# A fused attention and feed-forward kernel whose instructions are placed by a planner at build time, with a first batch in two query halves

## The chip, the cores and the metric

The kernel runs on one core of one Trainium2 chip. The metric is the device time in microseconds (us). The profile shows one execution; its span is about 1.8 us shorter than the time of the same run. Engines are written as in the profile: PE is TensorE, PEld its weight loads, DVE is VectorE, ACT is ScalarE, POOL is GpSimd, SP is SyncE. A tile is a named buffer; a bank is a piece of the memory that matmuls write to. The profile also records the clock that the array is granted, here full or half. "L84" is line 84 of the kernel that was profiled, so the numbers differ from one kernel to the next.

## The reference

Eight batches of squared-relu attention (12 heads, 448 tokens, head size 64), then an RMS norm and a gated feed-forward layer over 3584 tokens:

```python
scores = scale * np.matmul(q, k.transpose(0, 1, 3, 2))
attn = np.maximum(scores, 0.0) ** 2 / S
x = np.matmul(attn, v)                       # then heads side by side: 3584 x 768
xn = x / np.sqrt(np.mean(x * x, -1, keepdims=True) + 1e-06) * rms_g
g = xn @ w_gate                              # 768 -> 1536
out = (g * sigmoid(g) * (xn @ w_val)) @ w_out    # 1536 -> 768
```

## The kernel before

While the feed-forward layer of batch b runs on the PE, the attention of batch b+1 is put between its matmuls at fixed shares of the work. Nearly all matmuls use 64 of the 128 rows, so that two run side by side, one on each row half. Batch 0 has nothing to hide behind, so its whole attention and norm come first. Matmuls on zeros ("fillers", `psB`) keep the array busy there. All fillers of one call write one tile:

```python
def keep_busy(n):
    ps = ps_m.tile([P, S], FP32, name="psB", tag="mm")
    for _ in range(n):
        nc.tensor.matmul(out=ps[:], lhsT=ones_bf[:], rhs=busy_bf[:], start=True, stop=True)
...
keep_busy(16)
for _, fn in attention(0) + [(1.1, lambda: norm(0))]:
    fn()
keep_busy(24)
for nm in ("q", "k", "v"):
    load(nm, 1)
load_wo(0, 2)
load_wo(1, 2)
for b in range(B):
    ...                                # feed-forward of b, attention of b + 1 between
```

The norm of a batch is a square root on ACT, a reciprocal on DVE and six scalings on DVE:

```python
nc.scalar.activation(out=rstd[:], in_=psSS[:, :S], func=ACT.Sqrt, scale=1.0 / float(DM), bias=eps_col[:])
act_table(ACT.Silu)
nc.vector.reciprocal(out=rstd[:], in_=rstd[:])
```

Of the kernel before, what the change touches and what calls it, by code (L numbers as in the profile page):

```python
# [9 lines left out]
I32 = mybir.dt.int32  # L10
# [4 lines left out]
NCH = 4  # L15
U = 7
UH = 4


@with_exitstack  # L20
def kernel(
# [19 lines left out]
    assert HP == KT and (2 * S) % P == 0  # L41
    eps = 1e-6
    inv_attn = 1.0 / (float(D) * float(S))
    NT = 2 * S // P

# [6 lines left out]
    apool = ctx.enter_context(tc.tile_pool(name="attn", bufs=12))  # L52
    xpool = ctx.enter_context(tc.tile_pool(name="xT", bufs=1))
    npool = ctx.enter_context(tc.tile_pool(name="norm", bufs=2))
    hpool = ctx.enter_context(tc.tile_pool(name="hT", bufs=2))
    spool = ctx.enter_context(tc.tile_pool(name="sig", bufs=3))
    opool = ctx.enter_context(tc.tile_pool(name="ostage", bufs=3))
    ps_s = ctx.enter_context(tc.tile_pool(name="ps_s", bufs=2, space=bass.MemoryType.PSUM))
    ps_m = ctx.enter_context(tc.tile_pool(name="ps_m", bufs=4, space=bass.MemoryType.PSUM))
# [3 lines left out]
    ld = {}  # L63
    qkT = {}
    src_of = {"q": q, "k": k, "v": v}
    PE_T = 2

    def load(nm, b, h0=0, h1=H):
        runs = nm == "v" or b < PE_T
        n, w = (PC, NCH) if nm == "q" else (P, UH)  # L70
        if (nm, b) not in ld:
            shape = [n, H, w * D] if runs else [n, w, H * D]
            ld[nm, b] = ldpool.tile(shape, BF16, name=nm + "b", tag=nm + "b")
            if nm == "k" and runs:
                nc.vector.memset(ld[nm, b][D:, :, (UH - 1) * D :], 0.0)
        t = ld[nm, b]
        src = src_of[nm][b, h0:h1]
        if nm == "q":
            parts = [(slice(0, PC), PC, 0, NCH)]
        else:  # L80
            parts = [(slice(0, D), D, 0, UH), (slice(D, P), D, UH if nm == "k" else UH - 1, U)]
        for prt, n, u0, u1 in parts:
            if runs:
                nc.gpsimd.dma_start(  # L84
                    out=t[prt, h0:h1, : (u1 - u0) * D],
                    in_=src.rearrange("h (p u) d -> p h (u d)", p=n)[:, :, u0 * D : u1 * D],
                )
            else:
                to = t[prt].rearrange("p u (h d) -> p u h d", d=D)
                rows = src.rearrange("h (p u) d -> p u h d", p=n)  # L90
                step = u1 - u0 if nm == "q" else 1
                for u in range(u0, u1, step):
                    nc.gpsimd.dma_start(  # L93
                        out=to[:, u - u0 : u - u0 + step, h0:h1, :], in_=rows[:, u : u + step]
                    )

    def new_qkT(b):
        qkT[b] = qtpool.tile([P, HP, 2, S], BF16, name="qkT", tag="qkT")

    def transpose_dma(b):  # L100
        new_qkT(b)
        for c in range(UH):
            n = P if c < UH - 1 else D
            nc.sync.dma_start_transpose(
                out=qkT[b][:, :, 0, c * P : c * P + n], in_=ld["k", b][:n, c, :]
            )
        for c in range(NCH):
            nc.sync.dma_start_transpose(
                out=qkT[b][:, :, 1, c * PC : (c + 1) * PC], in_=ld["q", b][:, c, :]
            )  # L110

    wg_sb = wpool.tile([P, KT, F], BF16, name="wg_sb", tag="wg")
    wv_sb = wpool.tile([P, KT, F], BF16, name="wv_sb", tag="wv")
    wo_sb = wpool.tile([P, FT, DM], BF16, name="wo_sb", tag="wo")
    NSL = 4
    FS = F // NSL

    def load_w(which, s):
        dst, src = {"g": (wg_sb, moe_w_gate), "v": (wv_sb, moe_w_val)}[which]
        nc.gpsimd.dma_start(  # L120
            out=dst[:, :, s * FS : (s + 1) * FS],
            in_=src.rearrange("(kt p) f -> p kt f", p=P)[:, :, s * FS : (s + 1) * FS],
        )

    def load_wo(s, n):
        w = FT // n
        nc.gpsimd.dma_start(
            out=wo_sb[:, s * w : (s + 1) * w, :],
            in_=moe_w_out.rearrange("(fk p) m -> p fk m", p=P)[:, s * w : (s + 1) * w, :],
        )  # L130

    ones_bf = const.tile([P, P], BF16, name="ones_bf", tag="ones_bf")
    nc.vector.memset(ones_bf[:], 1.0)
    busy_bf = const.tile([P, S], BF16, name="busy_bf", tag="busy_bf")
    nc.vector.memset(busy_bf[:], 0.0)  # L135

    def keep_busy(n):
        ps = ps_m.tile([P, S], FP32, name="psB", tag="mm")
        for _ in range(n):
            nc.tensor.matmul(out=ps[:], lhsT=ones_bf[:], rhs=busy_bf[:], start=True, stop=True)  # L140

    load("q", 0, 0, 2)
    load("k", 0, 0, 2)
    ident = const.tile([P, P], BF16, name="ident", tag="ident")
    masks.make_identity(nc, ident[:])
    eps_col = const.tile([P, 1], FP32, name="eps_col", tag="eps_col")
    nc.vector.memset(eps_col[:], eps)
    scrap = const.tile([P, 1], FP32, name="scrap", tag="scrap")

    def act_table(func):  # L150
        nc.scalar.activation(out=scrap[:], in_=eps_col[:], func=func)

    act_table(ACT.Sqrt)
    g_sb = wpool.tile([P, KT], FP32, name="g_sb", tag="rmsg")
    nc.sync.dma_start(out=g_sb[:], in_=moe_rms_g.rearrange("(kt p) -> p kt", p=P))
    load("q", 0, 2, 6)
    load("k", 0, 2, 6)
    load("v", 0, 0, 6)
    load("q", 0, 6, 12)
    load("k", 0, 6, 12)  # L160
    load("v", 0, 6, 12)
    for s in range(NSL):
        load_w("g", s)
        load_w("v", s)

    behind = mybir.DependencyInfo(mybir.DependencyClass.Sync, mybir.DependencyReason.DATA)
    xTs = {}

    def transposes(b, j):
        if j == 0:  # L170
            new_qkT(b)
        psT = ps_m.tile([P, 2, S], BF16, name="psT", tag="mm")
        flat = psT[:].rearrange("p t s -> p (t s)")
        for nm, n, w, at in (("k", P, UH, 0), ("q", PC, NCH, S)):
            for c in range(w):
                for hh in range(2):
                    nc.tensor.transpose(  # L177
                        out=flat[hh * D : (hh + 1) * D, at + c * n : at + (c + 1) * n],
                        in_=ld[nm, b][:, 2 * j + hh, c * D : (c + 1) * D],
                        identity=ident[:n, :n],  # L180
                    )
        nc.vector.tensor_copy(out=qkT[b][:, j, :, :], in_=psT[:])

    rsq = {}
    pending = []

    def relu_on(b, j, c):
        return "dve" if c == UH - 1 or (b and j % 2 and c == 2) else "act"

    def square_on(b, j, c):  # L190
        return "pool" if b == 0 and j >= 3 and c == 1 else "dve"

    def flush():
        while pending:
            pending.pop(0)()

    def rectify(b, j, c, psS):
        r = apool.tile([P, 2, S], BF16, name="r", tag="r")
        if relu_on(b, j, c) == "dve":
            nc.vector.tensor_relu(out=r[:], in_=psS[:, :, :S])  # L200
        else:
            nc.scalar.activation(out=r[:], in_=psS[:, :, :S], func=ACT.Relu)  # L202
        eng = nc.gpsimd if square_on(b, j, c) == "pool" else nc.vector
        flush()
        pending.append(lambda: eng.tensor_tensor(out=r[:], in0=r[:], in1=r[:], op=ALU.mult))  # L205
        rsq[b, j, c] = r

    def scores(b, j, c):
        psS = ps_s.tile([P, 2, 512], FP32, name="psS", tag="psS")
        for hh in range(2):  # L210
            prt = slice(hh * D, (hh + 1) * D)
            nc.tensor.matmul(  # L212
                out=psS[:, hh, :S],
                lhsT=qkT[b][prt, j, 0, c * P : (c + 1) * P],
                rhs=qkT[b][prt, j, 1, :],
                start=True,
                stop=True,
            )
        rectify(b, j, c, psS)

    def rest_scores(b, j):

        psS = ps_s.tile([P, 2, 512], FP32, name="psS", tag="psS")
        for hh in range(2):
            prt = slice(hh * D, (hh + 1) * D)
            for jj in range(2):
                nc.tensor.matmul(  # L227
                    out=psS[jj * D : (jj + 1) * D, hh, :S],
                    lhsT=qkT[b][prt, j + jj, 0, (UH - 1) * P : (UH - 1) * P + D],
                    rhs=qkT[b][prt, j + jj, 1, :],  # L230
                    start=True,
                    stop=True,
                )
        return psS

    x2s = {}

    def attend(b, j, then=None):
# [35 lines left out]
        if then:  # L274
            rectify(*then, UH - 1, psR)
# [27 lines left out]

    xns, hTs = {}, {}

    class Stream:



# [270 lines left out]
```

## Time and profile before

| | before |
|---|---|
| time, median of 3 runs | 468.07 us (467.43 to 469.23) |
| span of the profiled run | 466.5 us |
| first projection matmul starts | 45.4 us |
| last matmul ends | 461.5 us |
| PE, DVE, ACT busy | 97%, 59%, 50% |

The page of the kernel before: the busy line, the chain that ended last, and two groups (busy us and mean ns of one after the bar, then the idle time before them):

```profile
PE 453.6 (97%) x5722; PEld 292.8 (63%) x5722; DVE 274.0 (59%) x403; ACT 234.9 (50%) x360; POOL 80.6 (17%) x97
...
PE 91%; DVE 3%; ACT 2%; DMA 1%; POOL 1%; issue 1%; POOLq 0%
...
L424 DVE RECIPROCAL rstd<-rstd 128x448 f32<-128x448 f32 x8 | 23.6, 2953 | 26.0 <-ACT rstd L420 26.0
...
L140 PE MATMUL psB<-busy_bf,ones_bf 128*128 128x448 bf16 x58 | 17.6, 418 | 1.3 <-DVE busy_bf L135 1.3
```

The timeline of the same run on PE (start us, length us, engine, line, what, count, and in brackets the idle time before it):

```profile
1.30 5.36 PE L140 MATMUL psB<-busy_bf,ones_bf 128*128 128x448 bf16 x16 [1.30 <-DVE busy_bf L135]
6.59 0.41 PE L177 MATMUL psT<-ident,kb 128*64 128x128 bf16 x8
...
9.59 0.64 PE L177 MATMUL psT<-ident,kb 128*64 128x128 bf16 x8 [2.39 <-DMA kb<-in_k_dram]
...
45.38 0.38 PE L441 MATMUL psP<-xn,wg_sb 128*64 128x448 bf16 x2
```

The same eight transposes take 0.41 us at 6.59 us, when the array's clock is full, and 0.64 us at 9.59 us, when the trace has it at half (from 9.1 to 19.4 us). PE is the chain, and it is busy 97% of the span. But that busy time contains 17.6 us on zeros, and the first useful projection starts only at 45.38 us.

Busy time does not tell how full the array is, because matmuls overlap. So I use one more measure, worked out from the start of every matmul in the trace. A matmul of N columns takes a slot, 189 ns for 448 columns, 109 ns for 256 and 96 ns for 224 (these are the spacings of adjacent starts). A matmul on half or a quarter of the array counts for half or a quarter of a slot. "Lost" is the length of a stretch less the slots of the useful matmuls that start in it. Fillers are not useful. The last matmul is counted to the end of its slot, 461.3 us before. Before, the useful slots sum to 405.6 us, and 33.8 us are lost before the first projection. A steady batch later loses only 2.4 to 2.9 us.

### The profile page before, as it was taken

What the parts mean: (1) busy time and instruction counts of PE and PEld (TensorE: products, weight loads), DVE (VectorE), ACT (ScalarE), POOL (GpSimd) and SP (SyncE); (2) the same over time, 40 slices, a digit from 0 to 9 for tenths busy, and PEclk for the clock granted to TensorE, in tenths of its full rate; (3) what the DMA queues carried; (4) which work ended last, traced back from release to release, by engine and by line L of the source; (5) the groups of instructions that cost most, each with busy time, mean ns of one, the idle gap of its engine ahead of it and who ended that gap; (6) DMA issues with size and microseconds to landing.
All of it is one profiled execution on the core that took longest, in us unless ns stands there. A gap on an engine that the chain in (4) does not pass through costs nothing.

```text
span 466.5 us, 12798 instructions
## 1 busy us (share of the span) xinstructions
PE 453.6 (97%) x5722; PEld 292.8 (63%) x5722; DVE 274.0 (59%) x403; ACT 234.9 (50%) x360; POOL 80.6 (17%) x97
## 2 busy tenths in 40 slices
PE   6989999999999999999999999999999999999995
PEld 3434655676666766676666766676667766676674
DVE  1676378866663867576566657576656677332200
ACT  1682246665645655375445755465535764532221
POOL 8438211571007000340007000100000000000000
PEclk8698999999999999999999999999999999999998
DMA  9999999799907970299209960438002200020013
GB/s 106 194 204 199 206 173 162 80 204 165 127 3 107 214 124 2 23 200 146 44 1 124 211 109 1 58 82 135 20 1 54 85 2 1 2 84 20 1 42 95
DMA packets 130758, 44.47 MB, mean 95 GB/s; under 512 B 102928, under 2 KB 127120, under 8 KB 130704
## 3 DMA queue, kind: packets, MB, share of 16 engines
q0 software_dynamic: 91648, 24.39, 54.1%
q1 hardware_dynamic: 39056, 19.28, 20.5%
q8 instruction: 44, 0.72, 0.6%
q14 instruction: 10, 0.08, 0.0%
HBM read 48.76 MB, written 11.01 MB: 128 GB/s over the span
## 4 chain that ended last, share of the span: by engine, by line
PE 91%; DVE 3%; ACT 2%; DMA 1%; POOL 1%; issue 1%; POOLq 0%
PE psP L380 47%; PE psO L380 23%; PE psAV L258 8%; PE psS L212 6%; PE psSS L380 2%; ACT r L202 2%; PE psB L140 1%; PE psT L177 1%; PE psS L227 1%; DMA kb<-in_k_dram 1%; DVE xn L427 1%; PE psP L441 1%; DVE r L200 1%; DVE r L205 1%; DVE rstd L424 1%
## 5 line engine op out<-in xcount | busy, mean ns | idle before, releaser
L380 PE MATMUL psP<-xn,wv_sb 64*128 64x448 bf16 x1140 | 229.0, 349 | 0.0
L380 PE MATMUL psP<-xn,wg_sb 64*128 64x448 bf16 x1128 | 227.8, 349 | 0.1
L380 PE MATMUL psO<-wo_sb,hT 64*128 64x256 bf16 x2016 | 139.6, 271 | 0.0
L202 ACT ACTIVATE r<-psS 128x896 bf16<-128x896 f32 x123 | 111.1, 918 | 47.5 <-PE psS L212 46.8
L380 PEld LDWEIGHTS <-wv_sb 64*128 64x128 bf16 x1140 | 96.1, 94 | 41.5 <-issue 4.3
L380 PEld LDWEIGHTS <-hT 64*128 64x128 bf16 x2016 | 101.1, 94 | 33.0 <-issue 2.9
L380 PEld LDWEIGHTS <-wg_sb 64*128 64x128 bf16 x1128 | 94.3, 94 | 35.6 <-issue 1.3
L205 DVE TENSOR_TENSOR r<-r 128x896 bf16<-128x896 bf16 x165 | 100.9, 628 | 16.3 <-ACT r L202 15.6
L456 DVE TENSOR_TENSOR hT<-sil,psP 128x448 bf16<-128x448 bf16 x96 | 59.5, 620 | 79.7 <-PE psP L380 52.4
L451 ACT ACTIVATE sil<-psP 128x448 bf16<-128x448 f32 x96 | 51.9, 542 | 74.7 <-PE psP L380 68.8
L200 DVE TENSOR_SCALAR r<-psS 128x896 bf16<-128x896 f32 x45 | 49.1, 1090 | 31.7 <-PE psS L227 24.2
L212 PE MATMUL psS<-qkT 64*128 64x448 bf16 x288 | 59.3, 358 | 1.9 <-DVE r L200 1.2
L490 ACT COPY ost<-psO 128x256 f32<-128x256 f32 x84 | 30.5, 372 | 43.5 <-PE psO L380 39.6
L276 ACT ACTIVATE xT<-psAV 128x896 bf16<-128x896 f32 x24 | 22.0, 917 | 54.4 <-PE psAV L258 50.1
L258 PE MATMUL psAV<-r,vb 64*64 64x448 bf16 x672 | 43.9, 361 | 1.8 <-POOL r L205 1.2
L84 POOL DMA_DIRECT2D vb<-in_v_dram x18 | 13.2, 750 | 167.7 <-PE psO L380 122.3
L424 DVE RECIPROCAL rstd<-rstd 128x448 f32<-128x448 f32 x8 | 23.6, 2953 | 26.0 <-ACT rstd L420 26.0
L93 POOL DMA_DIRECT2D kb<-in_k_dram x42 | 33.0, 1008 | 18.7 <-DMA wo_sb<-in_moe_w_out_dram 9.6
L258 PEld LDWEIGHTS <-vb 64*64 64x64 bf16 x672 | 17.3, 106 | 22.3 <-issue 10.3
L427 DVE SCALAR_TENSOR_TENSOR xn<-xT,g_sb,rstd 128x448 bf16<-128x448 bf16 x48 | 29.3, 680 | 0.3
L212 PEld LDWEIGHTS <-qkT 64*128 64x128 bf16 x288 | 19.8, 94 | 11.4 <-issue 6.2
L140 PE MATMUL psB<-busy_bf,ones_bf 128*128 128x448 bf16 x58 | 17.6, 418 | 1.3 <-DVE busy_bf L135 1.3
(38 smaller groups left out, 161.7 us busy)
## 6 DMA issues: line engine op xcount, KB each, us to landing
vb<-in_v_dram POOLq DMA_DIRECT2D x14, 384.0 KB, 7.2
qb<-in_q_dram POOLq DMA_DIRECT2D x7, 672.0 KB, 12.9
kb<-in_k_dram POOLq DMA_DIRECT2D x43, 96.0 KB, 12.7
out_dram<-ost SPq DMA_DIRECT2D x8, 336.0 KB, 4.1
wg_sb<-in_moe_w_gate_dram POOLq DMA_DIRECT2D x4, 576.0 KB, 16.5
wv_sb<-in_moe_w_val_dram POOLq DMA_DIRECT2D x4, 576.0 KB, 18.1
wo_sb<-in_moe_w_out_dram POOLq DMA_DIRECT2D x2, 1152.0 KB, 21.4
out_dram<-ost SPq DMA_DIRECT2D x8, 288.0 KB, 4.4
```

What stands on the lines that cost most here:

```text
L93: nc.gpsimd.dma_start(out=to[:, u - u0 : u - u0 + step, h0:h1, :], in_=rows[:, u : u + step])
L200: nc.vector.tensor_relu(out=r[:], in_=psS[:, :, :S])
L202: nc.scalar.activation(out=r[:], in_=psS[:, :, :S], func=ACT.Relu)
L205: pending.append(lambda: eng.tensor_tensor(out=r[:], in0=r[:], in1=r[:], op=ALU.mult))
L212: nc.tensor.matmul(out=psS[:, hh, :S], lhsT=qkT[b][prt, j, 0, c * P : (c + 1) * P], rhs=qkT[b][prt, j, 1, :], start=True, stop=True,)
L258: mm = nc.tensor.matmul(out=psAV[hh * D : (hh + 1) * D, jj, :S], lhsT=v[prt, 2 * (j + jj) + hh, u * D : (u + 1) * D], rhs=r[prt, hh, :], s ...
L380: mm = nc.tensor.matmul(out=self.ps[:, : self.w], lhsT=self.lhsT(i)[prt], rhs=self.rhs(i)[prt], start=(half == 0 and i == 0), stop=(half = ...
L424: nc.vector.reciprocal(out=rstd[:], in_=rstd[:])
L427: nc.vector.scalar_tensor_tensor(out=xn[:, kt, :], in0=xTs[b][:, kt, :], scalar=g_sb[:, kt : kt + 1], in1=rstd[:], op0=ALU.mult, op1=ALU.mult,
L451: nc.scalar.activation(out=s[:], in_=psG[:], func=ACT.Silu)
L456: nc.vector.tensor_tensor(out=hTs[b // 2][:, fb, o : o + S], in0=sil[b, fb][:], in1=psV[:], op=ALU.mult)
L490: nc.scalar.copy(out=ost[:, o : o + w], in_=ps[:, :w])
```

## The change

The intent is twofold. A planner with a model of every engine's times decides, while the kernel is built, in what order each engine gets its instructions and which engine takes a movable one. And batch 0 attends in two halves of 224 queries each: the first half is normed and goes through eight of the twelve pairs of projections before the second half is through. The diff has 1693 lines and rewrites the body of the kernel; this is its core, cut:

```diff
+class Bank:
+    def take(self, name, dtype=FP32, shape=None):
+        self.free = None
+        return self.pool.tile(shape or self.shape, dtype, name=name, tag=self.tag)
+class Planner:
+    SEM, PSUM, HAND, SW = 50.0, 210.0, 200.0, 95.0
...
+    def filler(self):
+        self.row()
+        s = max(self.t)
+        self.fill()
+        self.t = [s + 96.0, s + 96.0]
...
+    subs = [Sub(0, 0, HALF, 0.0), Sub(0, HALF, HALF, 0.0)]
+    subs += [Sub(b, 0, S, 0.0 if b < 2 else PACE) for b in range(1, B)]
...
+        cost = {"dve": dve_cost(2 * w, 0.52)}
+        if sub.b < 2:
+            cost["pool"] = 156.0 + 1.75 * 2 * w        # squares of batches 0 and 1
+        pl.task(PRIO_R, cost, square, [a], tok)
...
-        nc.vector.reciprocal(out=rstd[:], in_=rstd[:])
+                out=rstd[:, q0 : q0 + n], in_=rstd[:, q0 : q0 + n], func=ACT.Exp, scale=-0.5
...
+    def fill():
+        free = [x for x in wide + banks if x.free is not None and x.free <= max(pl.t)]
+        if not free:
+            return False
+        ps = free[0].take("psB")
+        o = ps[:, 0, :HALF] if free[0] in wide else ps[:, :HALF]
+        nc.tensor.matmul(out=o, lhsT=ones_bf[low, :], rhs=busy_bf[low, :], start=True, stop=True)
+        free[0].free = max(pl.t) + 96.0
+        return True
```

A filler is now 224 columns on the lower 64 rows, and every one takes a new tile of the first free bank. `Planner` assumes 96 ns for each.

## The prediction

> **What bounds it now.** A head, then a TensorE that hardly stops. In the timeline the first projection starts at 45.4 us, after the whole first batch: transposes from 6.6 us, scores, relu, squares, output, then a norm of sqrt, reciprocal (2.95 us on VectorE) and six scalings of 0.68 us. From 45.4 to 461.5 us TensorE is never named idle; copy and DMA end the span at 466.5 us. The chain of waits is 91% TensorE. I count each matmul as one row-tile slot: 189 ns (448 columns) or 109 ns (256), the spacing of adjacent starts in the timeline. The matmuls then fill 95% of each later period between first projections of consecutive batches (48.5 of 51.1 us), and 90% of 45 to 100 us. So the steady part can give about 2.5 us per batch; the head far more.
>
> **What changes.** The built order shows the same useful matmul work: 405.6 us of slots before, 406.0 after, without fillers. Batch 0 attends in two query halves; the first half's norm and first eight projection pairs come before the second half is through. Only 9.4 us of slots precede the first projection. The reciprocal becomes Ln and Exp: 0.6 us of Exp and a table load instead of 2.95 us. The Trainium skill (ScalarE: Activation LUTs, "What ACT_TABLE_LOAD costs") gives about 1283 ns per load; the trace shows 1283. Loads rise from 16 to 27. Each output-projection group hands over between row halves once, not twice; a handover costs two slots 11 ns each, so 84 fewer save about 2 us.
>
> **Head.** 57 fillers of 224 columns run first. The skill (TensorE: Matmul & The Clock Gate, Part 1) says the array starts at half clock, needing a busy window of about 3.4 us; the trace grants full clock at 5.7 us. At 187 ns cold and 96 ns warm they end near 9 us, 2 us later than the transposes start now. Half 1 then needs, by the order and the trace's durations (relu 0.92 or 1.09, square 0.62, copies 0.5 to 0.7, half widths 0.4 to 0.6), some 16 us on each of ScalarE and VectorE, plus about 3 us of waits: first projection at about 28.5 us (26 to 32) instead of 45.4.
>
> **After it.** 390.8 us of slots remain; at 95.5% 409 us. About 1.5 us more because 224-wide matmuls leave less time to load weights, and about 2 us because half 2's scaling (10 to 12 us of VectorE work) outlasts half 1's projections (about 10 us). Tail 5 us. Span 28.5 + 409 + 3.5 + 5 = 446; with the offset from span to time, 1.6 us, about 447; fewer handovers may take 1 to 2 us off: **446 us, range 440 to 454**. Chances: faster by over 2% 0.92, within 2% 0.06, slower 0.02.
>
> **What would show it.** Timeline: first gate projection at 26 to 32 us. Windows: slots fill 95 to 97% of the steady periods. Groups: no reciprocal; 27 table loads. Waits: TensorE waits about 2 us for scaling between 35 and 45 us. Last matmul to end of span still 5 us.
>
> **What would make it wrong.** A static order built on a model of time: if real fillers, DMAs or clock lag it, in-order engines stand; half-array fillers might not release the clock, moving the first projection past 32 us; half 2 could starve TensorE for 5 us or more; if the steady part lost more to placement than to switching and weight loads, the result is below 440.

## More of the kernel before

The squares of the scores go to POOL for three tiles of batch 0 only. POOL also issues all loads:

```python
def square_on(b, j, c):
    return "pool" if b == 0 and j >= 3 and c == 1 else "dve"
```

## The result, and the profile after

| | before | changed |
|---|---|---|
| time, median | 467.75 us (4 runs) | 492.61 us (4 runs, 492.58 to 495.26) |
| ratio, 95% interval | | 1.0549 (1.0495 to 1.0604) |
| span of the profiled run | 466.5 us | 490.8 us |
| first transpose on PE | 6.6 us | 23.7 us |
| first projection | 45.4 us | 59.9 us |

The change is 5% slower, where 5% faster was predicted.

The page of the changed kernel, the lines that answer to those of before. The last row is from its second part, PE clock in tenths by slices of 12.3 us:

```profile
PE 471.3 (96%) x6110; PEld 314.9 (64%) x6110; DVE 252.7 (51%) x413; ACT 260.7 (53%) x388; POOL 85.3 (17%) x100
...
PE 88%; DMA 4%; ACT 2%; issue 1%; DVE 1%; SPq 1%; POOL 1%; ACTq 0%
...
L1214 PE MATMUL psB<-busy_bf,ones_bf 64*128 64x224 bf16 x122 | 38.6, 322 | 6.9 <-DVE eps_col L390 1.2
...
PEclk9999989999899999999999999999999999999998
```

Its timeline in the head, PE lines, with two of the weight loads between the fillers:

```profile
1.18 22.56 PE L1214 MATMUL psB<-busy_bf,ones_bf 64*128 64x224 bf16 x57 [1.18 <-DVE eps_col L390]
...
1.58 0.10 PEld L1214 LDWEIGHTS <-ones_bf 64*128 64x128 bf16 x1 [0.30 <-issue]
1.98 0.10 PEld L1214 LDWEIGHTS <-ones_bf 64*128 64x128 bf16 x1 [0.29 <-issue]
...
23.67 0.64 PE L580 MATMUL psT<-ident,kb 128*64 128x128 bf16 x8
...
59.88 0.45 PE L138 MATMUL psg<-xn,wg_sb 64*128 64x224 bf16 x3
```

The 57 fillers last from 1.18 to 23.7 us: 396 ns each, not 96. The page calls PE busy in that time, and the list of waits names none, because the wait lies between two instructions of PE itself. The sign of it is the weight load that sits idle 0.30 us for "issue" before every filler. The built program says why: 112 of the 122 fillers wait on PE's own semaphore for the matmul just before. Two tiles of one bank follow each other, so the second must wait until the first is written and released.

The clock row is misleading here. The trace holds its first clock entry at 46.8 us, and the page shows full clock for the time before it. Yet eight transposes at 23.67 us take 0.64 us, as in the half-clock stretch of the kernel before (at 9.59 us), not 0.41 us. And the fillers themselves stand 396 ns apart there, but 308 ns at the end of the head, once the trace has full clock. I take it that the array ran at half clock until the first entry.

The waits of PE in the changed kernel (us in total, times, longest), and the chain behind the first of them (start us, us, what):

```profile
PE psR L735 <- DMA qkT<-qb: 4.8, 1, 4.8
PE psB L1214 <- DVE eps_col L390: 1.2, 1, 1.2
PE psS L714 <- DVE r L657: 1.0, 1, 1.0
```

```profile
98.43 1.78 POOL r L665
100.21 0.62 POOL kb L477
100.95 0.74 POOL kb L477
101.68 11.72 DMA qb<-in_q_dram
113.42 1.27 SPq L615
114.73 2.21 SPq L615
116.98 2.72 SPq L615
119.75 9.27 DMA qkT<-qb
129.05 0.59 PE psR L735 x4
```

Batch 2's q was loaded too late: its issue stands on POOL behind a square (`r L665`) of batch 1. A half-clock window begins as the stall ends, at 128.7 us.

Where the time went, in lost us by stretch (useful slots: 405.6 before, 406.0 in the others). Two repaired kernels of the experiments are shown with them:

| lost us | before | changed | E3 | E5 |
|---|---|---|---|---|
| until the first projection | 33.8 | 50.8 | 22.4 | 21.6 |
| to the first projection of batch 1 | 5.4 | 8.9 | 7.3 | 6.5 |
| to that of batch 2 | 2.9 | 9.0 | 9.5 | 2.7 |
| from there to the last matmul | 13.7 | 11.1 | 11.1 | 11.0 |
| after the last matmul | 5.2 | 5.1 | 5.2 | 5.2 |
| span | 466.5 | 490.8 | 461.4 | 453.1 |

The steady part did gain: the stretch from batch 2's first projection on loses 2.6 us less. The loss lies in the head (17.0 us), in the stretch after it (3.5) and in the one that holds the stall before batch 2's attention (6.1).

### The profile page after: what moved, and what is told of

Read it like the earlier page. It is cut to its first block, busy times and chain, and to the rows that moved or that the text cites. A ratio compares the mean times of both kernels' runs of the same rounds, so it can differ in the third digit from the quotient of the medians.

```text
span 490.8 us, 13609 instructions
## 1 busy us (share of the span) xinstructions
PE 471.3 (96%) x6110; PEld 314.9 (64%) x6110; DVE 252.7 (51%) x413; ACT 260.7 (53%) x388; POOL 85.3 (17%) x100
## 4 chain that ended last, share of the span: by engine, by line
PE 88%; DMA 4%; ACT 2%; issue 1%; DVE 1%; SPq 1%; POOL 1%; ACTq 0%
PE psv L138 22%; PE psg L138 21%; PE psO L138 20%; PE psB L1214 8%; PE psAV L821 8%; PE psS L714 6%; DMA qb<-in_q_dram 2%; DMA qkT<-qb 2%; PE psT L580 2%; PE psSS L138 2%; SPq L615 1%; PE psR L735 1%; DVE xn L920 1%; ACT r L659 1%; POOL r L665 0%
## 5 line engine op out<-in xcount | busy, mean ns | idle before, releaser
L138 PE MATMUL psg<-xn,wg_sb 64*128 64x448 bf16 (+1 forms) x1248 | 235.8, 338 | 0.5 <-DVE xn L920 0.5
L138 PE MATMUL psv<-xn,wv_sb 64*128 64x448 bf16 (+1 forms) x1248 | 235.2, 337 | 0.0
L665 DVE TENSOR_TENSOR r<-r 128x896 bf16<-128x896 bf16 (+1 forms) x166 | 101.5, 627 | 28.7 <-ACT r L659 28.1
L995 DVE TENSOR_TENSOR hT<-sil,psv 128x448 bf16<-128x448 bf16 x96 | 59.4, 619 | 56.1 <-PE psv L138 56.0
L982 ACT ACTIVATE sil<-psg 128x448 bf16<-128x448 f32 x96 | 52.0, 542 | 43.4 <-PE psg L138 43.2
L714 PE MATMUL psS<-qkT 64*128 64x448 bf16 (+1 forms) x324 | 62.6, 346 | 1.5 <-DVE r L657 1.0
L1214 PE MATMUL psB<-busy_bf,ones_bf 64*128 64x224 bf16 x122 | 38.6, 322 | 6.9 <-DVE eps_col L390 1.2
L821 PE MATMUL psAV<-r,vb 64*64 64x448 bf16 (+1 forms) x756 | 43.8, 340 | 0.3
L657 DVE TENSOR_SCALAR r<-psS 128x896 bf16<-128x896 f32 x22 | 23.9, 1089 | 28.1 <-PE psS L714 27.4
L920 DVE SCALAR_TENSOR_TENSOR xn<-xT,g_sb,rstd 128x448 bf16<-128x448 bf16 (+1 forms) x54 | 30.2, 627 | 5.8 <-ACT rstd L905 5.8
L821 PEld LDWEIGHTS <-vb 64*64 64x64 bf16 x756 | 18.7, 107 | 20.2 <-PE psAV L821 8.4
L1214 PEld LDWEIGHTS <-ones_bf 64*128 64x128 bf16 x122 | 12.4, 103 | 28.0 <-issue 26.2
```

The lines of the kernel that those rows point to most:

```text
L138: mm = self.nc.tensor.matmul(out=seg.bank["tile"][:, off : off + seg.w], lhsT=lhsT[prt], rhs=rhs[prt], start=(seg.first and h == 0 and i = ...
L657: nc.vector.tensor_relu(out=r[:, :, :w], in_=ps[:, :, :w])
L665: eng.tensor_tensor(out=r[:, :, :w], in0=r[:, :, :w], in1=r[:, :, :w], op=ALU.mult)
L714: nc.tensor.matmul(out=ps[:, hh, o : o + n], lhsT=t[prt, j, 0, c * P : (c + 1) * P], rhs=t[prt, j, 1, sub.q0 : sub.q0 + n], start=True, st ...
L821: mm = nc.tensor.matmul(out=ps[hh * D : (hh + 1) * D, jj, :n], lhsT=vt[prt, 2 * (ja + jj) + hh, u * D : (u + 1) * D], rhs=r[prt, hh, o : o ...
L920: nc.vector.scalar_tensor_tensor(out=xn[:, kt, q0 : q0 + n], in0=xTs[b, 0][:, kt, q0 : q0 + n], scalar=g_sb[:, kt : kt + 1], in1=rstd[:, q ...
```

## The experiments

The theories: (A) each filler waits for the one before, and that is the lost head. (B) The rival: fillers on half of the rows do not release the clock. (C) A second rival, the one that the prediction itself named: a static order lags the real machine everywhere, and the fillers are incidental. Later, for the stall: (D) POOL's squares hold up the loads; (E) other transfers at the same time slow them.

### E1 to E4: the wait and the rows, each alone and both; and no fillers

E1 keeps the tile while the bank's last user was a filler. Of 112 waits for PE itself 1 is left, and every other instruction keeps its place:

```diff
-        ps = free[0].take("psB")
+        ps = free[0].held if free[0].name == "psB" else free[0].take("psB")
```

> Same order on every engine as the changed kernel; the 122 half-array fillers keep one PSUM tile while nothing else used the bank, so 1 instead of 112 of them waits for the matmul before it. Theory A (each filler waits for the completion of the one before, 396 ns apart instead of 96 to 187): 57 fillers end at 7 to 12 us instead of 23.7, first gate projection at 29 to 36 us instead of 59.9, time 455 to 470 us (the 5 us wait for batch 2's transposed q may grow). Rival B (the 64-row fillers never release the clock, whatever their spacing): fillers end at 11 to 12 us, transposes still take 0.64 us per eight, clock full only from 35 us or later, time 465 to 475. Rival C (the static order as such lags, fillers incidental): time stays above 485.

E2 leaves the waits and uses all rows; E3 has both edits:

```diff
-        nc.tensor.matmul(out=o, lhsT=ones_bf[low, :], rhs=busy_bf[low, :], ...)
+        nc.tensor.matmul(out=o, lhsT=ones_bf[:], rhs=busy_bf[:], ...)
```

> Same order, fillers use all 128 rows, and each still takes a new tile and so waits for the one before. Theory A: 57 fillers still take 15 to 23 us, first gate projection at 45 to 60 us, time 478 to 493. Rival B (half-array fillers are what kept the clock at half until 46.8 us): clock full before 10 us, transposes 0.41 us per eight, time 470 to 485.

> Both mended: full-array fillers in one tile. Theory A and B together: fillers end at 8 to 12 us, clock full by 8 us and held, first gate projection at 27 to 32 us, time 448 to 462 with the wait for batch 2's transposed q at 5 us or more. If A alone matters, equal to the half-array version within 3 us. Rival C: above 485.

E4 has no fillers:

```diff
     def warm():
...
-        return 0 not in started
+        return False
```

> No fillers at all; the array waits for its data. Theory A: transposes start at 6.5 to 7.5 us; clock at half through most of the head; first gate projection at 30 to 37 us; time 452 to 470. Rival B (the clock matters more than the fillers' own time): time 475 or more, because the whole head runs at half clock. Rival C: above 485.

| | fillers' rows | wait | time us | ratio to before | clock first full at | first transpose | first projection |
|---|---|---|---|---|---|---|---|
| changed | 64 | yes | 492.61 | 1.0549 | 46.8 us | 23.7 | 59.9 |
| E1 | 64 | no | 471.43 | 1.0074 | 15.4 us | 11.9 | 34.4 |
| E2 | 128 | yes | 496.79 | 1.0633 | 48.7 us | 23.9 | 62.2 |
| E3 | 128 | no | 462.82 | 0.9901 | 6.9 us | 9.5 | 31.5 |
| E4 | none | | 463.64 | 0.9900 | 16.4 us | 6.4 | 29.5 |

The heads of E1, E2 and E3, in this order, from their timelines:

```profile
1.18 10.79 PE L1217 MATMUL psB<-busy_bf,ones_bf 64*128 64x224 bf16 x57 [1.18 <-DVE eps_col L393]
11.90 0.64 PE L583 MATMUL psT<-ident,kb 128*64 128x128 bf16 x8
```

```profile
22.78 1.14 PE L1214 MATMUL psB<-busy_bf,ones_bf 128*128 128x224 bf16 x3
23.86 0.64 PE L580 MATMUL psT<-ident,kb 128*64 128x128 bf16 x8
```

```profile
1.18 8.37 PE L1217 MATMUL psB<-busy_bf,ones_bf 128*128 128x224 bf16 x57 [1.18 <-DVE eps_col L393]
9.48 0.41 PE L583 MATMUL psT<-ident,kb 128*64 128x128 bf16 x8
```

A holds. Taking the wait away takes 21.2 us off (492.61 to 471.43), with every instruction in its old place, so C cannot explain the slowdown. The rows alone (E2) gain nothing: with the wait, fillers on all rows do not release the clock either, until 48.7 us. So B fails as the rival cause. It is a second, smaller cause once the wait is gone: E3 beats E1 by 8.6 us, with the clock full at 6.9 us instead of 15.4, and the transposes at 0.41 instead of 0.64 us. E4 says how bad the fillers of the changed kernel are: without any it is 29 us faster than with them. Three expected times were missed by a little: E1 lies 1.4 us above A's range, E3 1 us, and E2 4 us. The stall is still in all four: waits of 4.2 to 7.3 us in their profiles.

### E5 and E6: the late load of batch 2

E5 is E3 with batch 1's squares off POOL:

```diff
-        if sub.b < 2:
+        if sub.b < 1:
             cost["pool"] = 156.0 + 1.75 * 2 * w
```

> Full-array fillers in one tile (462.8 us before this) and, besides, batch 1's squares never on GpSimd, whose queue also issues the loads. Theory D (batch 2's loads stand behind those squares in GpSimd's order, so the transposed q is 5.6 us late and the stall costs a half-clock window): the q load is issued at 52 to 60 us instead of 71.7, no wait of TensorE on it, no clock drop at 99 us; time 453 to 458. Rival E (the transfers of batch 3's loads, running at the same time, make the q load and the transposes slow): q still 2 us or more late, time 459 to 463.

E6 is E3 with batch 3's loads planned 20 us later:

```diff
-            load_later(b + 2, [Tok(max(pl.t))])
+            load_later(b + 2, [Tok(max(pl.t) + (20000.0 if b == 1 else 0.0))])
```

> Full-array fillers in one tile, and batch 3's loads planned 20 us later, squares left on GpSimd. Rival E: q load of batch 2 takes 8 to 10 us instead of 12.6 and its last transpose 4 to 5 us instead of 8.9; wait under 1 us; time 455 to 459. Theory D alone: the load still starts at 71 us, the wait shrinks by 2 us at most; time 460 to 463.

E5: 455.05 us (4 runs, 454.49 to 455.30), ratio 0.9721 (0.9703 to 0.9738), 7.8 us less than E3. POOL in E3 and then in E5, the square and the loads of batch 2:

```profile
68.40 1.78 POOL L668 TENSOR_TENSOR r<-r 128x896 bf16<-128x896 bf16 x1 [5.23 <-ACT r L662]
70.14 1.53 POOL L480 DMA_DIRECT2D kb<-in_k_dram  x2
71.65 2.31 POOL L480 DMA_DIRECT2D qb<-in_q_dram  x1
```

```profile
58.48 0.75 POOL L480 DMA_DIRECT2D kb<-in_k_dram  x1 [4.82 <-DMA wo_sb<-in_moe_w_out_dram]
64.80 2.27 POOL L480 DMA_DIRECT2D qb<-in_q_dram  x1 [5.58 <-PE psAV L824]
```

And the longest wait of PE in E3, then in E5:

```profile
PE psR L738 <- DMA qkT<-qb: 5.4, 1, 5.4
```

```profile
PE psS L717 <- ACT xT L849: 1.4, 1, 1.4
```

The q load is issued 6.85 us sooner (71.65 to 64.80). The wait of 5.4 us is gone, and with it the half-clock window that E3's trace has at 99.0 us. The load itself is no faster: it lands 12.6 us after its issue in E3 (at 84.2 us) and 12.4 us after it in E5 (at 77.2). But the four transposes of q that follow it are faster. Their line in the DMA view of E3 and then of E5 (the last number is the median us from issue to landing):

```profile
qkT<-qb SPq DMA_TRANSPOSE x4, 9.1
```

```profile
qkT<-qb SPq DMA_TRANSPOSE x4, 5.6
```

The last of them lands at 99.55 us in E3 and at 87.27 in E5. Of these 12.3 us, 7.0 come from the earlier load, which is D. The other 5.2 come from faster transposes: in E3 five loads of batch 3 are issued at 75.1 to 79.2 us, just before them, and in E5 these loads come only from 85.4 us on, after the last of the transposes was issued (84.5). That is what E would lead to. As an estimate from these numbers, either part alone would have covered nearly all of the wait of 5.4 us. So E5 shows what the squares on POOL cost in this plan, but not how much of it goes by D and how much by E. The Trainium skill (TensorE: Matmul & The Clock Gate, Part 1, on engine queue depths) gives GpSimd strict FIFO order, per core of that engine; this case agrees: the load stood behind a square that itself waited 5.23 us. E5's load came later than I expected (52 to 60 us), since something else then held it until 64.8.

E6 failed as an experiment. The order of POOL's instructions came out the same as E3's, and the loads of batch 3 still followed directly. At 463.63 us (ratio 0.9913) it is in effect a repeat of E3, with a wait of 7.2 us in its profile. It was meant to part D from E, so that question stays open.

### E7, E10: the first batch whole

E7 is E3 with one sub-batch for batch 0 and one norm; E10 has the squares off POOL too, so it compares with E5.

```diff
-    subs = [Sub(0, 0, HALF, 0.0), Sub(0, HALF, HALF, 0.0)]
+    subs = [Sub(0, 0, S, 0.0)]
...  (loads of q, transposes and the projections' order go with it)
```

> Full-array fillers in one tile and the planner, but the first batch attends whole, with one norm and full-width projections. If the halves are worth what the prediction gave them (first projection about 17 us sooner, some 10 us of it paid back by work that moves behind it): first projection at 40 to 46 us, time 468 to 476. If the planner alone carries the gain: within 3 us of 462.8.

> The first batch whole, with the q load no longer late. If the two halves are worth about what they save in lost time (22.4 + 16.8 us lost up to batch 3 with halves, 27.3 + 10.9 + 1.5 without, both with a wait of 5 us): time 456 to 460, first projection at 39 to 41 us, no wait for the transposed q. If the halves matter more: 461 to 468.

E7: 464.54 us, ratio 0.9931, first projection at 40.2 us. E10: 458.04 us, ratio 0.9788 (0.9763 to 0.9812), first projection at 39.7 us. So the halves bring the first projection 9 us forward (30.8 in E5) but are worth only 3.0 us in the end (458.04 to 455.05), because the second half's attention and more lost time follow it: E5 loses 6.5 us in the next stretch, E10 4.8. My first range for E7 (468 to 476) was too high; the other one, within 3 us of 462.8 if the planner alone carries the gain, held. Most of the gain of the repaired kernels is not that of the halves: E10 is 10.2 us below the 468.26 us of the kernel before in its rounds. That is the rest of the diff, the planned order and the norm without the reciprocal among it; no run separates these.

### E8: the wait put into the kernel before

```diff
         for _ in range(n):
+            if last is not None:      # wait for the completion of the filler before
+                tc.add_manual_dep(nc.tensor.nop().ins, last.name, ...)
-            nc.tensor.matmul(out=ps[:], ...)
+            last = nc.tensor.matmul(out=ps[:], ...).ins
```

> The kernel before, with nothing changed but that each filler of a run of fillers waits for the one before it. Theory A: the first 16 take about 9 us instead of 5.4 (585 ns apart cold), the 24 ahead of the first projection about 8 to 9 us instead of 4.7 if warm and 13 if cold; first projection at 50 to 58 us instead of 45.4; time 473 to 482. If the wait costs nothing by itself: 466 to 470.

E8: 475.47 us, ratio 1.0145 (1.0116 to 1.0174). Its first fillers and transposes, to be compared with 5.36 and 0.41 us before:

```profile
1.29 9.73 PE L144 MATMUL psB<-busy_bf,ones_bf 128*128 128x448 bf16 x16 [1.29 <-DVE busy_bf L135]
10.96 0.64 PE L181 MATMUL psT<-ident,kb 128*64 128x128 bf16 x8
```

The fillers stand 613 ns apart at half clock instead of 373, and 423 ns at full clock instead of 189. The first projection comes at 53.0 us instead of 45.4, and the clock is full only from 21.4 us instead of 5.7. After the head, every stretch loses the same as before, within 0.2 us. So the wait costs this much in a kernel without the planner as well; it shows A independently of everything else in the change. The size is E8's own: here the weight load also stands behind the wait, and in the changed kernel it does not.

### E9, E11, E12: how much the fillers are worth

All three start from E5. E9 puts the fillers back on 64 rows, with the tile kept. E11 plans 150 ns for a filler, which leaves 37 before the first transpose and 79 in all. E12 has none. The edits in this order:

```diff
-        nc.tensor.matmul(out=o, lhsT=ones_bf[:], rhs=busy_bf[:], ...)
+        nc.tensor.matmul(out=o, lhsT=ones_bf[low, :], rhs=busy_bf[low, :], ...)
```

```diff
-        self.t = [s + 96.0, s + 96.0]
+        self.t = [s + 150.0, s + 150.0]
```

```diff
-        return 0 not in started
+        return False
```

> The kernel of 455.05 us (full-array fillers in one tile, batch 1's squares off GpSimd) with its fillers back on 64 rows; the tile is still kept. Theory B' (64 rows release the clock later: 15.4 us against 4.4 to 6.9 us in the profiles so far): clock full at 10 to 20 us, fillers end at 10 to 12 us instead of 8.5, first projection 2 to 4 us later, time 457 to 465. If the rows do not matter and the earlier difference was the phase of the clock's windows: 454 to 457 and clock full by 8 us.

> The kernel of 455.05 us, planned with 150 ns for a filler instead of 96, so 37 instead of 57 fillers come first and 79 instead of 122 in all. If the first fillers still outlast the arrival of data: first transpose at 6.5 to 7.5 us instead of 8.7, time 452.5 to 454.5. If the clock falls to half for it: 455 to 460.

> The kernel of 455.05 us without any filler. Theory: the head is bound by ScalarE and VectorE, so a half clock there costs little: first projection at 29 to 31 us, time 453 to 458. If a half clock matters: 459 or more.

| | time us | ratio to before | first projection | half clock after its first release, in the profile |
|---|---|---|---|---|
| E5 | 455.05 | 0.9721 | 30.8 us | none until the end |
| E9 | 461.01 | 0.9862 | 37.2 us | none, but first full at 22.0 us |
| E11 | 455.74 | 0.9737 | 29.7 us | 29.8 to 36.6 us |
| E12 | 457.01 | 0.9763 | 29.7 us | 24.6 to 34.8 us |

E9 confirms the rows by themselves: 6.0 us, and in both profiles with fillers on 64 rows and no wait the clock was released only after the first run of fillers had ended at 12.0 us (at 15.4 and 22.0 us, against 4.4 to 6.9 us in all seven profiles with fillers on 128 rows and no wait: E3, E5, E6, E7, E10, E11 and E13). E11 came out in its second range: its first projection came 1 us sooner, but the half clock then fell into the projections, and the stretch to batch 1 lost 10.5 us instead of 6.5. E12 shows the same without fillers. Good fillers are worth about 2 us here (457.01 to 455.05, in different rounds), and 0.8 us, within the noise, from E4 to E3; those of the changed kernel cost 29 (463.64 in E4 to 492.61).

### E13, E14: what was left open

E13 is E5 with only the first run of fillers shortened to 37. E14 is the changed kernel with only E5's edit, the squares.

```diff
-        self.t = [s + 96.0, s + 96.0]
+        w = 96.0 if self.real else 150.0      # real: set by the first transpose
+        self.t = [s + w, s + w]
```

> The kernel of 455.05 us, with 37 instead of 57 fillers before the first transpose and the later ones planned at 96 ns as there (65 of them). If the clock fell in the trimmed kernel because the later fillers thinned out (65 to 42): clock held at full from about 6 us, first transpose at 7 us, first projection at 29 to 30 us, time 453 to 454.5. If a shorter first run alone is enough to lose the clock: a half-clock window between 20 and 40 us, time 455 to 458.

> The changed kernel as it stands, fillers untouched, only batch 1's squares taken off GpSimd. Theory D holds without the filler repair too: no wait of TensorE for the transposed q, saving 5 to 9 us: 484 to 488. If the fillers' delay is what makes the loads late here: within 2 us of 492.6.

E13: 453.91 us, ratio 0.9712 (0.9683 to 0.9742), the best of all, but its interval overlaps that of E5. Its profile has the first transpose at 6.4 us, and one half-clock window from 31.8 to 35.2 us. So whether the thinner later fillers or the shorter first run cost E11 the clock is not settled: E11 lost two windows and E13 one, in one profile each. E6 lost the same window (31.8 to 35.2 us) with all 122 fillers. The mean clocks say that it comes and goes: one window takes 0.004 off the mean. E13's two slower runs (455.12 and 455.51 us) have 0.994, and its three faster ones (453.06 to 453.91 us) 0.997 to 0.998, a clock too high for such a window.

E14: 484.99 us (4 runs), ratio 1.0374. The wait on `qkT<-qb` is gone from PE's waits. The edit saves 7.6 us with the bad fillers and 7.8 us with the good ones, so the two causes add: 29.8 us for the fillers (changed to E3) and 7.8 us for the squares (E3 to E5). As in E5, q both landed sooner (113.4 to 103.2 us) and was transposed faster after that (from 15.6 us to about 11).

## Why the prediction was wrong

The prediction was 446 us (440 to 454), and 492.61 us was measured. Point by point:

- **"At 187 ns cold and 96 ns warm they end near 9 us" failed.** This is the step that broke it. The step priced a filler at its throughput and left out the wait for the one before; without the wait the 57 do end at 9.5 us (E3). The 57 fillers took 396 ns each and ended at 23.7 us, and 56 of the 65 later ones waited as well. The first projection came at 59.9 us instead of 28.5. E1 to E4 and E8 show the wait as the cause, and E3, with neither wait nor half rows, has its first projection at 31.5 us, inside the predicted 26 to 32. The wait could have been read in the built program before the run: 112 of 122 fillers carry a semaphore wait on PE.
- **"The trace grants full clock at 5.7 us" was carried over and failed.** That was the clock of fillers without waits. With the wait it was full at 46.8 us. The text had named half-array fillers as a risk; they are real (8.6 us from E1 to E3, 6.0 us from E5 to E9) but not the main cause.
- **"After it": the late q load of batch 2 was missing from the sum.** Nothing in the text puts a price on POOL's squares in front of the loads. Taking the squares off is worth 7.8 us in E5 and 7.6 us in E14.
- **"390.8 us of slots remain" was an arithmetic slip.** 406.0 less 9.4 is 396.6; I had taken the fillers off twice. E5 has 396.9 us of useful slots after its first projection.
- **The rest of the sum held where it could be tested.** E5 loses 20.2 us from its first projection to the last matmul, where 18 and 3.5 were expected, and has a tail of 5.2 us, where 5 were. With the slip corrected the sum gives about 452 us of span; E5 has 453.1. That this is so close is partly luck: E5's first projection is 2.3 us later than predicted, and the rest 1.7 us shorter; and E5 is not the kernel that was predicted.
- **Smaller steps.** The table loads are 27, as predicted, and 1283 ns each. The steady periods fill 96.8% (47.9 of 49.5 us), in the predicted range. A wait on `xn` of about 2 us was expected and 0.5 us found. The loss of 1.5 us to weight loads at 224 columns does not exist: adjacent starts stand 96 ns apart (median), as the slot. The saving at hand-overs was about right: where output-projection matmuls follow each other (intervals under 150 ns), a slot takes 110.8 ns on average in the changed kernel against 112.7 before. That makes 1.9 us over 1008 slots.
- **The worth of the halves was overrated.** The text makes 17 us of the earlier projection. In E5 against E10 the halves are worth 3.0 us.

## What to carry to other kernels

Before trusting a build-time plan, compare its assumed cost with the built program: an instruction that the plan costs at its throughput may carry a wait for its predecessor's completion, and a fresh tile in the same buffer is enough to make one. Filler matmuls need the same care as useful ones, since here bad ones cost 29 us and good ones earned 2 at most. Keep compute that can be late off a queue that must issue early loads.

## What the Trainium skill lacked or had wrong

- TensorE: Matmul & The Clock Gate, Part 1, says that a busy window of about 3.4 us releases the clock and that idle windows take it back. It does not say how much work in a window counts as busy. Here 57 fillers that waited for each other, 396 ns apart where 187 ns is the spacing without the wait, did not release it in 22.5 us, and with the later ones among the useful matmuls it was full only at 46.8 us (E2, on all rows: 48.7 us).
- The same page does not say that the rows count. Dense fillers on 64 rows, from 1.2 to 12.0 us, did not release the clock while they ran (full at 15.4 and 22.0 us); on 128 rows it was full at 4.4 to 6.9 us.
- The same page, "Single matmul latency", gives (219 + N)/1.2 ns cold, so 369 ns for N = 224 and 556 for 448. The spacing of fillers that wait for each other was 396 ns (E2, on all rows: 400) and 613 ns, 27 (31) and 57 ns more; the last has an extra wait instruction, with the weight load behind it. I found no figure there for a matmul that waits for the one before.
- The same page, "LDWEIGHTS", gives about P/1.2 ns, 107 ns for 128 columns. Loads of 64 rows and 128 columns took 94 ns on average in the trace of the kernel before (2016 loads of `hT`).
- I found no page that warns that a profile can show full clock where it has no clock record yet (a general caution about clock events in traces is there): the first entry of the changed kernel's trace is at 46.8 us, and the transposes' 0.64 us per eight told the truth.
